# Summing most of block A's output projection in four strips, in a decode attention kernel

## The chip, the cores and the metric

The kernel runs on one core of one Trainium2 chip. The metric is the device time of one execution in microseconds (us); a value quoted for a kernel is the median of its executions. Before the change it was 1328.24 us (three executions, 1328.06 to 1329.07).

## The reference, cut to what matters

Two attention blocks with one query each. Block A reads the whole key and value caches of 32 heads; block B reads only the last 4096 keys of 8 heads, each shared by 4 query heads. Each block ends with a projection by a 4096 x 512 matrix `wo`; the results are concatenated.

```python
# A: H = 32, Sk = 32768, Dh = 128, D = 512      B: the same with 8 kv heads and a window of 4096 keys
q = (x @ wq).reshape(B, Sq, H, Dh).transpose(0, 2, 1, 3)
scores = einsum("bhqd,bhkd->bhqk", q, k_cache) * Dh ** -0.5
p = softmax(scores)
o = einsum("bhqk,bhkd->bhqd", p, v_cache)
a = o.transpose(0, 2, 1, 3).reshape(B, Sq, H * Dh) @ wo
# result: concatenate([a, b], axis=-1), 1024 values
```

Block A's caches are 32 heads x 2 x 8.39 MB in bf16. That is nearly all of the 570 MB that the kernel reads.

## The kernel before

PE is the matmul engine, DVE the vector engine, ACT the scalar engine; SP issues the loads. In this kernel the loads go to SBUF, the matmuls write to the banks of PSUM. The program gives each engine its own list of operations. An operation names the ones it depends on, and a helper turns that into semaphores. In a loop over A's 32 heads, PE transposes keys, DVE copies them out of PSUM, PE makes the scores, ACT the exponential, and PE the sum over the values. The loads are issued from SP, as soon as the buffer they go to is free. After the loop come the two projections. `wo` is loaded in parts: two for B, five for A, the last ones small so that little work is left behind the last byte.

```python
WO_CUTS = {"A": (0, 11, 19, 25, 29, 32), "B": (0, 16, 32)}     # in chunks of 128 rows of wo

def proj_part(self, name, part, out):
    a0, a1 = self.WO_CUTS[name][part:part + 2]
    oz, wo = self.c[name]["oz"], self.kbuf[:, HALF * DH * self.wo_third(name):]
    def mm(e):
        inst = None
        for a in range(a0, a1):
            inst = out(e, oz[:, a:a + 1], wo[:, 512 * a:512 * a + 512], a)
        return inst
    return self.op("pe", mm, (self.wosem[name][part], 16), self.c[name]["ozop"])   # waits for its load

def halves(self, e, bank, lhsT, rhs, begin, end):               # one chunk as two matmuls of 256 columns
    for i in range(2):
        inst = e.matmul(bank[64 * i:64 * i + 1, 0:256], lhsT=lhsT, rhs=rhs[:, 256 * i:256 * i + 256],
                        start=begin, stop=end, tile_position=(0, 64 * i), skip_group_check=True)
    return inst
```

The projection of B puts chunk `a` as one matmul of 512 columns into strip `a % 4` of a bank. It then has to add the four strips: a DVE copy of the bank to SBUF, and two f32 matmuls (four records in the trace) that sum its rows. The projection of A used the halves for every chunk, and needs no such step. (`...` marks cuts in the code of this document.)

## Time and profile before

| | before |
|---|---|
| median of 3 | 1328.24 us |
| span of the profiled execution | 1326.0 us |
| read from memory, rate over the span | 570.43 MB, 430 GB/s |
| PE, DVE, ACT busy | 73%, 57%, 4% |
| last weights landed, span ended | 1323.02, 1326.0 us |

The lines behind this table are in the prediction below. In the page, "busy" is a share of the span, and the DMA row gives tenths of each of 40 slices. In the timeline, a row is the start, the length, the engine, the source line and the operation with its count; a bracket says how long the engine stood idle before it and what ended that. Lengths of matmuls overlap: a row of 32 strips took 1.90 us, where one alone takes 0.379.

### The profile page before, as it was taken

To read this page: it belongs to the slowest core of one execution; us is meant where nothing else is said; L and a number is where in the kernel's file an instruction comes from. 1 tells how busy PE (TensorE), PEld (TensorE's weight loads), DVE (VectorE), ACT (ScalarE), POOL (GpSimd) and SP (SyncE) were. 2 spreads that over 40 slices of the span, in tenths; PEclk is the share of its full clock that TensorE was granted. 3 is DMA by queue.
4 is the path that set the end of the run, shared out by engine and by line. 5 is a ranking of instruction groups with operands and counts; after the bars stand their busy time and mean duration, and the time that the engine had idled before them with its cause. 6 is when DMAs were issued, how large, how long until landed. Compare 5 with 4: busy or idle time off the path is not lost. (4 is left out here: it accounts for less than half of the span.)

```text
span 1326.0 us, 28874 instructions
## 1 busy us (share of the span) xinstructions
PE 967.7 (73%) x13260; PEld 676.0 (51%) x13260; DVE 753.0 (57%) x1350; ACT 54.8 (4%) x167; POOL 2.2 (0%) x17
## 2 busy tenths in 40 slices
PE   4657678786777877676787767678776767877686
PEld 3445446554444655444465544455554445555453
DVE  4645456665545666554666655466655546665563
ACT  0000000000000000000000000000000000000000
POOL 0000000000000000000000000000000000000000
PEclk8878898878779887877988787898888789888888
DMA  9999999999999999999999999999999999999998
GB/s 403 445 420 427 427 431 439 437 427 435 441 427 433 435 433 433 433 437 429 435 437 429 435 435 433 431 435 437 429 433 435 435 433 433 433 431 435 435 433 351
DMA packets 13350, 570.63 MB, mean 430 GB/s; under 512 B 1812, under 2 KB 1816, under 8 KB 2200
## 3 DMA queue, kind: packets, MB, share of 16 engines
q1 hardware_dynamic: 13048, 570.44, 99.7%
q8 instruction: 9, 0.15, 0.0%
q10 hardware_dynamic: 288, 0.00, 0.0%
q14 instruction: 5, 0.04, 0.0%
HBM read 570.43 MB, written 0.00 MB: 430 GB/s over the span
## 5 line engine op out<-in xcount | busy, mean ns | idle before, releaser
L564 DVE COPY kt<-psT 128x1024 bf16<-128x1024 bf16 x1056 | 655.4, 684 | 238.9 <-PE psT L560 237.4
L560 PE MATMUL psT<-ident,kbuf 128*128 128x128 bf16 x8448 | 579.9, 234 | 170.2 <-DMA kbuf<-in_A_k_cache_dram 157.4
L560 PEld LDWEIGHTS psT<-ident,kbuf 128*128 128x128 bf16 x8448 | 540.3, 106 | 262.3 <-DMA kbuf<-in_A_k_cache_dram 165.5
L663 PE MATMUL psACC<-vbuf,ptsb 128*4 128x512 bf16 (+1 forms) x2112 | 187.5, 532 | 22.8 <-ACT ptsb L638 22.0
L583 PE MATMUL psS<-kt,qw 128*32 128x512 bf16 x2048 | 158.3, 386 | 14.8 <-DVE kt L564 14.8
L677 DVE TENSOR_SCALAR oc_A<-psACC,hot_A 128x128 f32<-128x128 f32 x32 | 11.2, 351 | 252.0 <-PE psG L690 252.0
L663 PEld LDWEIGHTS psACC<-vbuf,ptsb 128*4 128x4 bf16 (+1 forms) x2112 | 60.2, 111 | 140.3 <-issue 93.9
L611 ACT ACTIVATE psb<-psS,nb_A 128x512 bf16<-128x512 f32 x32 | 22.0, 687 | 1171.3 <-DVE nb_A L610 1171.3
L583 PEld LDWEIGHTS psS<-kt,qw 128*32 128x32 bf16 x2048 | 34.1, 95 | 57.4 <-DVE kt L564 30.4
L690 PE MATMUL psG<-oc_A,hw 128*32 128x128 f32 (+1 forms) x128 | 19.3, 227 | 52.3 <-DVE oc_A L679 52.3
L690 PEld LDWEIGHTS psG<-oc_A,hw 128*32 128x32 f32 x128 | 11.4, 109 | 62.5 <-DVE oc_A L679 55.1
L635 PE MATMUL psPT<-ident,psb 128*128 128x128 bf16 x136 | 17.9, 274 | 34.0 <-ACT psb L611 34.0
L679 DVE SCALAR_TENSOR_TENSOR oc_A<-psACC,hot_A,oc_A 128x128 f32<-128x128 f32 x96 | 33.7, 351 | 3.4
L600 DVE TENSOR_REDUCE tr_in<-psS 128x1 f32<-128x512 f32 x34 | 23.5, 692 | 17.8 <-PE psS L583 17.8
L635 PEld LDWEIGHTS psPT<-ident,psb 128*128 128x128 bf16 x136 | 10.2, 118 | 37.1 <-ACT psb L611 36.7
L604 PE MATMUL psACC<-rows,tr_in 128*1 128x64 f32 x64 | 8.7, 217 | 25.6 <-DVE tr_in L600 25.6
L638 ACT ACTIVATE ptsb<-psPT 128x512 bf16<-128x512 bf16 x34 | 20.3, 597 | 30.4 <-PE psPT L635 30.4
L604 PEld LDWEIGHTS psACC<-rows,tr_in 128*1 128x1 f32 x64 | 2.7, 81 | 35.7 <-DVE tr_in L600 35.7
L608 PE MATMUL psACC<-mr_A,nscale 1*128 1x1 f32 x64 | 12.1, 256 | 9.8 <-DVE mr_A L607 9.8
L608 PEld LDWEIGHTS psACC<-mr_A,nscale 1*128 1x128 f32 x64 | 9.4, 182 | 15.7 <-DVE mr_A L607 15.7
L610 DVE COPY nb_A<-psACC 128x1 f32<-128x1 f32 x32 | 5.0, 157 | 15.0 <-PE psACC L608 15.0
L607 DVE TENSOR_REDUCE mr_A<-psACC 1x1 f32<-1x64 f32 x32 | 6.8, 212 | 11.7 <-PE psACC L604 11.7
(80 smaller groups left out, 73.7 us busy)
## 6 DMA issues: line engine op xcount, KB each, us to landing
kbuf<-in_B_k_cache_dram SPq DMA_DIRECT2D x2, 4096.0 KB, 32.0
vbuf<-in_B_v_cache_dram SPq DMA_DIRECT2D x2, 4096.0 KB, 25.3
kbuf<-in_A_k_cache_dram SPq DMA_DIRECT2D x2, 4096.0 KB, 22.8
vbuf<-in_B_wq_dram SPq DMA_DIRECT2D x1, 4096.0 KB, 12.5
vbuf<-in_A_wq_dram SPq DMA_DIRECT2D x1, 4096.0 KB, 32.0
kbuf<-in_B_wo_dram SPq DMA_DIRECT2D x2, 2048.0 KB, 32.6
kbuf<-in_A_wo_dram SPq DMA_DIRECT2D x1, 1408.0 KB, 25.7
kbuf<-in_A_wo_dram SPq DMA_DIRECT2D x1, 1024.0 KB, 27.9
```

The costliest lines, as they stand in the source:

```text
L560: inst = e.transpose(T[:, 128 * k:128 * k + 128], src[:, DH * k:DH * k + DH], self.ident[:, :])
L564: self.copies.append(self.op("dve", lambda v: v.tensor_copy(KT[:, :], T[:, :]), o, to="pe"))
L583: inst = e.matmul(self.S[32 * c:32 * c + 32, :], lhsT=win, rhs=self.kt[(bb + c // 2) % NKT][:, 512 * (c % 2):512 * (c % 2) + 512], start=b ...
L600: o = dve(lambda v: v.reduce_max(tr["in"][:, 0:1], self.S[:, :], axis=AXX), self.sdone, self.k_pool, to="pe" if name == "A" else None)
L604: o = self.op("pe", lambda e: e.matmul(self.ACC[0:1, 0:64], lhsT=tr["in"][:, 0:1], rhs=self.rows64[:, :], start=True, stop=True, skip_grou ...
L608: o = self.op("pe", lambda e: e.matmul(self.ACC[:, 64:65], lhsT=self.nscale[:, :], rhs=t["mr"][0:1, :], start=True, stop=True, skip_group_ ...
L611: self.sread = self.op("act", lambda s: s.activation(out=self.psb[:, :], in_=self.S[:, :], func=ACTF.Exp, bias=t["nb"][:, k:k + 1], scale= ...
L635: inst = e.transpose(PT[:, 128 * jj:128 * jj + 128], self.psb[:, 128 * jj:128 * jj + 128], self.ident[:, :])
L638: self.ptread = self.op("act", lambda s: s.activation(out=self.ptsb[:, :], in_=PT[:, 0:512], func=ACTF.Copy), self.psread, to="pe")
L663: inst = e.matmul(acc[32 * c:32 * c + rows, 0:512], lhsT=lhsT, rhs=rhs, start=begin, stop=end, tile_position=(0, 32 * c), skip_group_check ...
L679: o = self.op("dve", lambda v, src=src, hot=hot: v.scalar_tensor_tensor(out=oc, in0=src, scalar=hot, in1=oc, op0=ALU.mult, op1=ALU.add), p ...
L690: return self.op("pe", lambda e: e.matmul(self.G[0:32, c0 + c:c0 + c2], lhsT=win, rhs=t["oc"][g % len(t["oc"])][:, c:c2], start=False, sto ...
```

## The change

The intent is to take matmuls out of the end of the kernel. Three quarters of A's chunks are summed in four whole-width strips as B's are, which takes one matmul per chunk instead of two. The strips are added up ahead of the last two loads, and the last seven chunks are summed in halves on top of that. One dependency in the loop is dropped as well: the exponential of a head no longer names the gather, a small operation on PE, of the head before.

```diff
@@ emit_stats: the exponential of one head
-                accum_out=t["oc"][k][:, DH:DH + 1]), o, self.psread, self.gath if g else None, to="pe")
+                accum_out=t["oc"][k][:, DH:DH + 1]), o, self.psread, to="pe")
@@ emit_proj
-        for part in range(len(self.WO_CUTS["B"]) - 1):
-            o = self.proj_part("B", part, lambda e, lhsT, rhs, a: e.matmul(
-                self.S[32 * (a % 4):32 * (a % 4) + 1, :], lhsT=lhsT, rhs=rhs, start=(a < 4), stop=(a >= 28),
-                tile_position=(0, 32 * (a % 4)), skip_group_check=True))
-        strips = self.op("dve", lambda v: v.tensor_copy(self.pb[:, :], self.S[:, :]), o)
-        o = self.op("pe", lambda e: self.halves(e, self.ACC, self.e32[:, 0:1], self.pb, True, True), strips, self.accread)
-        self.store("B", self.ACC, 512, o)
-        for part in range(len(self.WO_CUTS["A"]) - 1):
-            o = self.proj_part("A", part, lambda e, lhsT, rhs, a: self.halves(e, self.PT, lhsT, rhs, a == 0, a == 31))
+        free = None
+        for name, cut, bank, to in (("B", 2, self.S, self.ACC), ("A", 3, self.T[1], self.PT)):
+            whole = name == "B"
+            top = self.WO_CUTS[name][cut]
+            for part in range(cut):
+                o = self.proj_part(name, part, lambda e, lhsT, rhs, a, bank=bank, top=top: e.matmul(
+                    bank[32 * (a % 4):32 * (a % 4) + 1, :], lhsT=lhsT, rhs=rhs, start=(a < 4), stop=(a >= top - 4),
+                    tile_position=(0, 32 * (a % 4)), skip_group_check=True))
+            strips = self.op("dve", lambda v, bank=bank: v.tensor_copy(self.pb[:, :], bank[:, :]), o, free)
+            o = free = self.op("pe", lambda e, to=to, whole=whole: self.halves(e, to, self.e32[:, 0:1], self.pb, True, whole),
+                               strips, self.accread)
+            if whole:
+                self.store("B", self.ACC, 512, o)
+        for part in range(3, len(self.WO_CUTS["A"]) - 1):
+            o = self.proj_part("A", part, lambda e, lhsT, rhs, a: self.halves(e, self.PT, lhsT, rhs, False, a == 31))
         self.store("A", self.PT, 0, o)
```

## The prediction

> **What bounds the kernel now.** I read the page from the top: the busy shares, the 40 slices, the queues, then the chain that ended last. After that I took the stages in a table of windows, the loads with their time to landing, and the last 12 us as a timeline.
>
> ```profile
> PE 967.7 (73%) x13260; PEld 676.0 (51%) x13260; DVE 753.0 (57%) x1350; ACT 54.8 (4%) x167; POOL 2.2 (0%) x17
> ...
> DMA  9999999999999999999999999999999999999998
> ...
> HBM read 570.43 MB, written 0.00 MB: 430 GB/s over the span
> ...
> DMA 2%; PE 1%; SPq 0%; issue 0%; DVE 0%
> ```
>
> No compute engine is over 73% busy, but the DMA row is 9 in every slice except the last. The kernel reads 570 MB once, and 570.43 MB at 430 GB/s is the whole span of 1326 us. From the table of windows, the steady part:
>
> ```profile
> 45.00:1255.00 1210.00, 894.14 (x12252) 628.30 (x12251) 694.42 (x1224) 49.65 (x155) 0.00 (x0) 0.83 1.00 433
> ```
>
> Of 1210 us, PE is busy 894, DVE 694, and the DMA share is 1.00 at 433 GB/s. The loads of a head are not late either: an 8 MB key load (8.39 MB) at 433 GB/s needs 19.4 us by itself, and the view of loads gives it 27.7 us from issue to landing, a value load 26.4 us. So a load is issued 7 to 8 us before its predecessor has finished (27.7 - 19.4 and 26.4 - 19.4). Anything in the loop that is shorter than some 7 us leaves the queue full.
>
> Only the end is left, after the last byte. The chain of waits there (start, length, what):
>
> ```profile
> 1292.35 0.04 issue
> 1292.39 30.63 DMA kbuf<-in_A_wo_dram
> 1323.02 0.04 issue
> 1323.06 0.51 PE psPT L725 x6
> 1323.57 0.02 issue
> 1323.60 0.42 DVE out_sb L731
> ```
>
> The last weight load of block A is issued at 1292.39, queues behind everything else and lands at 1323.02. Six matmuls (its three chunks, two halves each), one DVE cast and the store follow; the span ends at 1326.0. The timeline shows what PE did before that:
>
> ```profile
> 1314.71 1.90 PE L738 MATMUL psS<-kbuf,oz_B 128*1 128x512 bf16 x32
> 1316.66 0.69 DVE L741 COPY pb<-psS 128x512 f32<-128x512 f32 x1 [1.65 <-PE psS L738]
> 1317.41 0.60 PE L725 MATMUL psACC<-pb,e 128*1 128x256 f32 x4 [0.80 <-DVE pb L741]
> 1317.84 2.24 PE L725 MATMUL psPT<-kbuf,oz_A 128*1 128x256 bf16 x38
> 1320.75 0.82 PE L725 MATMUL psPT<-kbuf,oz_A 128*1 128x256 bf16 x12 [0.67 <-DMA kbuf<-in_A_wo_dram]
> 1321.98 0.60 PE L725 MATMUL psPT<-kbuf,oz_A 128*1 128x256 bf16 x8 [0.41 <-DMA kbuf<-in_A_wo_dram]
> 1323.06 0.49 PE L725 MATMUL psPT<-kbuf,oz_A 128*1 128x256 bf16 x6 [0.48 <-DMA kbuf<-in_A_wo_dram]
> ```
>
> The brackets decide the case: PE stands idle 0.67, 0.41 and 0.48 us ahead of the third, fourth and fifth loads, each time for a DMA. It has already caught up with the loads, so there is no backlog for the change to shorten.
>
> [...] 32 strip matmuls took 1.90 us, one of them 0.379 us, hence (1.90 - 0.379)/31 = 49 ns each, although each has 512 columns. [...]
>
> **The change part by part.**
>
> (1) The exponential on ACT no longer names the previous head's gather among its dependencies. [...] Per head, ACT loses one wait that was long satisfied, and PE perhaps one semaphore increment. In the trace ACT starts 0.03 us after the DVE copy that releases it (copy 1303.41 + 0.16, activation 1303.60). At most 0.03 us of a head's 39 us, against 7 us of lead: zero.
>
> (2) Block B's projection: the same 32 strips, copy and halves, with unchanged flags. Zero.
>
> (3) Block A, removed: 25 chunks x 2 halves = 50 matmuls of 256 columns. They cost (2.24 - 0.272)/37 = 53 ns each, or 106 ns a chunk, 2.7 us in all. Added: 25 strips of 512 columns at 49 ns, 1.2 us; one DVE copy of 128x512 f32, 0.69 us; and four f32 half records. These took 0.60 us in B, and there the next bf16 matmul started 0.43 us after the first of them (1317.41 to 1317.84). PE records: 13260 - 50 + 25 + 4 = 13239; DVE one more, 1351.
>
> The schedule that follows, with loads landing as now. Parts 0 and 1 (19 chunks) are done by about 1319.7: the second load is in by 1318.9 (issued 1290.96, 27.9 us), and eight strips take 7 x 0.049 + 0.379 = 0.72. PE then waits about 1 us for part 2. That starts at 1320.75, and six strips end 5 x 0.049 + 0.379 = 0.62 later, at 1321.37. The DVE copy starts 0.05 later, as after B's strips, at 1321.42, and ends at 1322.11. The f32 halves start 0.06 later at 1322.17 (B: 1317.35 to 1317.41). Part 3's eight matmuls, whose weights landed at 1321.9, now stand behind them: they start at 1322.17 + 0.43 = 1322.60 instead of 1321.98. At about 50 ns each, PE is ready for part 4 at 1323.00. Part 4 lands at 1323.02 and starts at 1323.06, as now.
>
> So part 3 is **0.6 us later, and the end does not move**: the margin I work out is 0.06 us. If one of my terms is short by 0.1 us, the last six matmuls slip by some 0.05 us. Cast and store are the same instructions. Sum: 1.5 us less matmul time, none on the path; 0.7 us of copy and the halves added, just off the path or touching it by 0 to 0.2 us. Expected: +0.05 us in 1328.24, or 0.004%.
>
> **Rivals.**
>
> The copy and the f32 halves become the new wait. They put a serial step from PE to DVE to PE between part 2 and part 3, and my margin of 0.06 us is smaller than my error. If the f32 records hold PE for their whole 0.60 us rather than 0.43, part 4 starts at about 1323.2 and the time is 0.15 us more. Should the copy also start late, 0.3 us more: 1328.5.
>
> PE's clock falls. The changed kernel leaves PE idle for about 1 us before part 2 and 0.7 us during the copy. In 1300 to 1310 the granted clock was 0.68, in the last 8 us it was 1.00. Were it to fall again, matmuls on the path would take some half longer: the f32 halves, part 3 and part 4 would together slip by about 0.5 us. Against it: the tail of now has idle stretches of 0.4 to 0.8 us at 1.00. Time then: 1328.8.
>
> PE had been the bound at the end and the strips gain. That would need a backlog. The whole possible gain from PE is the stretch from landing to the last matmul's end, 0.51 us, and the change leaves those six matmuls as they are. Gain 0.
>
> The loop speeds up because ACT is released earlier. A head would have to be limited by that chain, but PE sits idle 5.06 us at the start of a head waiting for keys (the timeline around 626 us), and the DMA row has no hole. Gain 0.
>
> **Range and chances.** Every path but a broken one lies within -0.1 and +0.6 us. What is left is the spread between executions: three of the kernel before went from 1328.06 to 1329.07. I predict 1328.3 us. The range, 1327.0 to 1329.7, allows about 1 us of spread either way plus the rivals. 2% would be 26.6 us, and nothing here has that size: the whole tail behind the last load is 3 us. Faster 0.01, within 2% 0.98, slower 0.01.
>
> **What would show it right or wrong.** Right: the DMA share and the 433 GB/s of the steady part are unchanged. The chain still ends with the load of block A's last weights, six matmuls, cast and store, with the same 3.0 us from landing to end. The copy of the second strip bank starts near 1321.4 from the span's start (give or take a shift of the whole trace). Part 3's matmuls name the DVE copy or the f32 halves as what held them, no longer a DMA, and PE's idle ahead of part 4 shrinks from 0.48 us to almost nothing. Wrong in a step: the last six matmuls start more than 0.1 us after their landing (then the copy is on the path), or the granted clock in the last 6 us is below 1.00. Wrong altogether: a hole in the DMA row in the loop, which would mean that the removed wait moved the release of a buffer, or a last load that lands at another time because the queue is filled differently.

49 ns a strip comes from the 1.90 us above and 0.69 us for the copy from the trace, so 1.5 us less matmul time, none of it on the path, and 0.7 us of copy and the halves just off it come to +0.05 us. The result stays right, the runs show: wait_only, with the dropped wait alone, is correct, and so is after_again, which sums chunks 25 to 31 on top of the strips' halves. In the changed kernel's trace the gather of the head before ended 23.3 us or more before each exponential. "Some half longer" at a lower clock is the estimate, beside a clock of 0.68; in after_again, at 0.50, the last 14 matmuls took 1.70 us for 0.93.

## The result, and the profile after

The changed kernel took **1328.32 us** (six executions, 1327.73 to 1328.88), the kernel before in the same rounds 1328.66 (1328.06 to 1329.3). The ratio is **0.9997**, with a 95% interval of 0.9984 to 1.001. Ratios here divide the mean time of one kernel's fast executions by that of the other's of the same rounds, so they are not quite the ratio of the medians.

From the page of the changed kernel, the busy shares and the DMA row; then the steady part from its table of windows (busy time of PE, weight loads, DVE, ACT, POOL, then PE's granted clock as the profile gives it, 1.00 being the full one, the DMA share and GB/s):

```profile
PE 965.5 (73%) x13239; PEld 676.2 (51%) x13239; DVE 754.4 (57%) x1351; ACT 54.8 (4%) x167; POOL 2.2 (0%) x17
...
DMA  9999999999999999999999999999999999999998
```

```profile
45.00:1255.00 1210.00, 893.53 (x12263) 630.57 (x12260) 695.73 (x1225) 49.69 (x155) 0.00 (x0) 0.83 1.00 433
```

The counts are the predicted ones: PE 21 records fewer, DVE one more. In all the trace has 28802 instructions for 28874. The difference of 72 is 21 matmuls and 21 weight loads less, one copy more, and 31 waits less on ACT, one for each head but the first. The stream is as before, 433 GB/s at a share of 1.00.

The end is where the chain of waits changed (start, length, what):

```profile
1290.47 29.99 DMA kbuf<-in_A_wo_dram
1320.46 0.04 issue
1320.50 0.61 PE psT L742 x6
1321.12 0.02 issue
1321.14 0.70 DVE pb L745
1321.84 0.04 issue
1321.89 1.38 PE psPT L725 x18
1323.27 0.02 issue
1323.29 0.42 DVE out_sb L731
```

The chain no longer starts from the fifth load of A but from the **third**. Its six strips, the copy, and then 18 records in one piece: the four f32 halves, eight matmuls of the fourth load and six of the fifth. The fifth load was issued at 1291.42 and took 31.3 us, so it landed at 1322.72. PE reached its matmuls at about the same moment, since the last six take 0.5 us and end at 1323.27. From that landing to the last cast it is 0.57 us, before it was 0.58 (1323.02 to 1323.60). So the copy and the sums of the strips are on the chain now, and in this execution they cost nothing.

### The profile page after: what moved, and what is told of

The parts are those of the page before. It is cut to its first block, busy times and chain, and to the rows that moved or that the text cites. A ratio compares the mean times of both kernels' runs of the same rounds, so it can differ in the third digit from the quotient of the medians.

```text
span 1326.1 us, 28802 instructions
## 1 busy us (share of the span) xinstructions
PE 965.5 (73%) x13239; PEld 676.2 (51%) x13239; DVE 754.4 (57%) x1351; ACT 54.8 (4%) x167; POOL 2.2 (0%) x17
## 5 line engine op out<-in xcount | busy, mean ns | idle before, releaser
L663 PE MATMUL psACC<-vbuf,ptsb 128*4 128x512 bf16 (+1 forms) x2112 | 184.0, 524 | 23.0 <-ACT ptsb L638 22.0
L583 PE MATMUL psS<-kt,qw 128*32 128x512 bf16 x2048 | 157.6, 385 | 15.0 <-DVE kt L564 15.0
## 6 DMA issues: line engine op xcount, KB each, us to landing
kbuf<-in_B_wo_dram SPq DMA_DIRECT2D x2, 2048.0 KB, 33.1
kbuf<-in_A_wo_dram SPq DMA_DIRECT2D x1, 1408.0 KB, 26.3
```

Of the source, the lines that this page charges most:

```text
L583: inst = e.matmul(self.S[32 * c:32 * c + 32, :], lhsT=win, rhs=self.kt[(bb + c // 2) % NKT][:, 512 * (c % 2):512 * (c % 2) + 512], start=b ...
L663: inst = e.matmul(acc[32 * c:32 * c + rows, 0:512], lhsT=lhsT, rhs=rhs, start=begin, stop=end, tile_position=(0, 32 * c), skip_group_check ...
```

## The experiments

They came on three chips, each compared with runs of the kernel before on the same chip. The table gives all of them; "distance" is from the landing of the last weights (issue of the fifth load plus its time to landing) to the start of the last cast, in the profiled execution, and "clock" is the granted TensorE clock over that distance.

| run | median us | ratio to before (95%) | distance us | clock |
|---|---|---|---|---|
| before (first profile) | 1328.24 | | 0.58 | 1.00 |
| changed kernel (first profile) | 1328.32 | 0.9997 (0.9984 to 1.001) | 0.57 | 1.00 |
| after_again | 1329.06 | 0.9999 (0.9982 to 1.0015) | 2.12 | 0.50 |
| before_again | 1328.92 | 1.001 (0.9994 to 1.0025) | 0.58 | 1.00 |
| wait_only | 1328.19 | 0.9993 (0.9977 to 1.001) | 0.57 | 1.00 |
| few_chunks | 1328.76 | 0.9998 (0.9981 to 1.0014) | 1.78 | 0.50 |
| cut19 | 1328.55 | 0.9996 (0.9979 to 1.0012) | 1.51 | 0.50 |
| strips32 | 1329.71 | 1.0006 (0.9989 to 1.0022) | 2.50 | 0.50 |
| copies6 | 1332.97 | 1.0027 (1.001 to 1.0044) | 5.37 | 0.50 from 1324.6 |
| no_marks | 1328.28 | 0.9994 (0.9977 to 1.0011) | 2.20 | 0.50 |
| half_v | 1325.18 | 0.9969 (0.9952 to 0.9985) | 2.19 | 0.50 |
| pv_half_more | 1332.99 | 1.0026 (1.0009 to 1.0043) | 3.99 | 0.50, then 1.00 |
| pv_thrice | 1408.39, one run, state unknown | | | |
| warm | 1328.68 | 1.0002 (0.9989 to 1.0016) | 0.70 | 1.00 |

The row before_again is the yardstick: the very same kernel came out at 1.001 against itself. A microsecond is not to be seen in these times, only in traces.

### Is the copy now on the path? after_again

No edit; the changed kernel once more.

> The changed kernel once more, for a second trace of it. All theories: 1328.4 us within 1.3 us, the same as before. My theory (the last load sets the end, PE is just caught up when it lands): from the landing of the last weight load of block A to the start of the last cast 0.5 to 0.7 us, as in the kernel before (0.58). Rival (the copy and the f32 halves are now the wait): that distance is over 0.8 us in this second trace.

The time was the same, 0.9999. The trace was not; it gave the rival its number. The end of its timeline:

```profile
1319.56 1.02 PE L742 MATMUL psT<-kbuf,oz_A 128*1 128x512 bf16 x8 [2.10 <-DMA kbuf<-in_A_wo_dram]
1321.44 1.02 PE L742 MATMUL psT<-kbuf,oz_A 128*1 128x512 bf16 x6 [0.86 <-DMA kbuf<-in_A_wo_dram]
1322.50 0.69 DVE L745 COPY pb<-psT 128x512 f32<-128x512 f32 x1 [5.24 <-PE psT L742]
1323.25 1.02 PE L725 MATMUL psPT<-pb,e 128*1 128x256 f32 x4 [0.79 <-DVE pb L745]
1324.05 1.70 PE L725 MATMUL psPT<-kbuf,oz_A 128*1 128x256 bf16 x14
1325.80 0.42 DVE L731 CAST out_sb<-psPT 65x256 bf16<-65x256 f32 x1 [2.60 <-PE psPT L725]
```

The DVE copy is as long as ever, but every group of matmuls is slower: the 14 last ones took 1.70 us where the first trace of the same kernel has 0.93, the f32 records 1.02 where B's took 0.60. The table of windows says why (the columns as above; the third from the end is the granted clock):

```profile
1318.20:1319.20 1.00, 0.00 (x0) 0.00 (x0) 0.00 (x0) 0.00 (x0) 0.00 (x0) 1.00 0.97 399
1319.20:1320.20 1.00, 0.64 (x8) 0.10 (x8) 0.00 (x0) 0.00 (x0) 0.00 (x0) 0.62 1.03 420
1320.20:1322.20 2.00, 1.14 (x10) 0.10 (x6) 0.00 (x0) 0.00 (x0) 0.00 (x0) 0.50 0.95 357
```

PE had stood idle for 2.10 us waiting for A's second load, and its clock fell to 0.50. The last load landed at 1290.98 + 32.7 = 1323.68, the last cast started at 1325.80. What goes with such a fall can be read from the clock records. In the traces of the kernel before and of the changed kernel, all 268 stretches at one clock that lie within the span last a whole number of 3.413 us, to within 0.001 us. So I cut the traces into windows of that length. In the first trace of the changed kernel the clock came up at 1309.36 and fell at 1326.43, five windows later; in after_again it fell at 1319.45. Here is the last window before that, and below it the corresponding one of the first trace:

```profile
1316.04:1319.45 3.41, 1.27 (x15) 0.28 (x15) 0.52 (x2) 0.00 (x0) 0.00 (x0) 1.00 1.01 414
1316.19:1319.60 3.41, 1.85 (x23) 0.50 (x23) 0.54 (x2) 0.00 (x0) 0.00 (x0) 1.00 1.01 410
```

In after_again PE was busy for 1.27 us of the window, because A's second load landed 0.1 us after its end. In the first trace that load came in time: 1.85 us, and 1.73 in the next window. The kernel before has 2.67 and 1.91. From 60 us on, in the traces of these two kernels, all 126 windows at full clock with less than 1.63 us of work lost it, all 348 with more than 2.07 kept it, and of 15 in between 12 kept it. At half clock, none of 118 windows with less than 2.71 us brought it back, and all 124 with more than 2.73 did. Other traces agree: worked out from their timelines and tables of windows, the last 3.41 us before the fall held about 0.6 us (copies6), 0.8 (few_chunks), 1.2 (no_marks), 1.4 (cut19 and strips32) and 1.5 (pv_half_more). So the full clock of the first trace was a near thing.

What grew is not a wait for a semaphore: between the third load's landing (1321.40) and the last cast there are 4.40 us for the 2.83 of the first trace. The strips are 0.43 us longer (1.04 for 0.61) and the 18 records 1.15 (2.53 for 1.38), together the difference.

### The dropped wait alone: wait_only

```diff
-   ... o, self.psread, self.gath if g else None, to="pe")       # in the kernel before
+   ... o, self.psread, to="pe")
```

> The kernel before with the one dependency of the exponential dropped and nothing else. My theory: 1328.5 us within 1.3 us, idle of PE for key loads as before (157 us in all), and only ACT's instruction count falls, by 31. Rival (the removed wait releases ACT and with it the buffers earlier): 1 us faster or more (31 heads x 0.03 us), and loads with a longer time to landing than 27.7 and 26.4 us.

The trace has 28843 instructions, 31 fewer. The idle time of PE for key loads is 157.6 us (before 157.4), the times to landing are 27.6 and 26.3 us (27.7 and 26.4). The time is 0.9993 with an interval from 0.9977 to 1.001: the same. The rival's 1 us is smaller than this interval, so it is the unchanged waits that speak against it, not the time.

### What can a faster sum win at all? few_chunks and cut19

few_chunks sums only four chunks of each of A's first three loads (a wrong result, wrong by 32%).

```diff
-            for a in range(a0, a1):
+            for a in range(a0, a0 + 4 if name == "A" and part < 3 else a1):
```

> The changed kernel with only 4 chunks of each of block A's first three loads summed (12 instead of 25; a wrong result on purpose, all loads and waits kept). My theory: the same time, 1328.4 us within 1.3 us, because PE's sums are done while the next load is under way: what any faster sum of these chunks could win is bounded by this. Rival (PE's sums ahead of the last loads cost time): faster by the 0.6 us of 13 strips, and by more if PE had a backlog.

The time was the same (0.9998). PE spared 13 strips, waited longer instead, 2.50 us for the second load and 1.30 for the third, and fell to half clock as well:

```profile
1319.04 0.59 PE L742 MATMUL psT<-kbuf,oz_A 128*1 128x512 bf16 x4 [2.50 <-DMA kbuf<-in_A_wo_dram]
1320.93 0.59 PE L742 MATMUL psT<-kbuf,oz_A 128*1 128x512 bf16 x4 [1.30 <-DMA kbuf<-in_A_wo_dram]
```

The time alone could not show the 0.6 us at stake (its interval is 2.5 us down to 1.9 us up), and the low clock costs this run over 1 us behind the last load. It is the waits that show it: less work ahead of these loads only turns into waiting for them, so the gain of the change had nowhere to come from.

cut19 moves the sum of the strips one load forward.

```diff
-        ... ("A", 3, self.T[1], self.PT)):
+        ... ("A", 2, self.T[1], self.PT)):
-        for part in range(3, len(self.WO_CUTS["A"]) - 1):
+        for part in range(2, len(self.WO_CUTS["A"]) - 1):
```

> The changed kernel with 19 instead of 25 chunks in strips: copy and halves then stand behind the second load of block A and not the third. My theory: the same time (1328.4 us within 1.3 us), but PE waits again ahead of the last three loads (0.3 us or more ahead of the last), and the chain that ended last goes straight from the last load into its six matmuls. Rival (strips in themselves cost or save): the time moves with the number of chunks in strips.

The time was the same (0.9996), but my picture of the trace was wrong. PE did not wait ahead of the last three loads. It had waited 0.72 us for the first and 1.61 for the second load, which landed only at 1321.62; the clock fell to 0.50, the strips' sum took 1.8 us, and then all 13 chunks of the last three loads ran in one stretch of 26 matmuls in 2.98 us. The distance was 1.51 us.

### The size of the margin: copies6 and strips32

copies6 makes the copy of A's strips six times in a row.

```diff
+            for _ in range(0 if whole else 5):
+                o = self.op("dve", lambda v, bank=bank: v.tensor_copy(self.pb[:, :], bank[:, :]), o, free)
             strips = self.op("dve", ...
```

> The changed kernel with the copy of block A's strip bank made six times in a row, each waiting for the one before. My theory (the chain strips, copy, halves, part 3 already fills all the time up to the last landing): nearly all of 5 x 0.7 us shows, +3.3 to +3.8 us, so 1331.7 to 1332.2 us, and the last load waits in the buffer for as long. Rival (a wide hidden margin in front of the last load): under +1 us. Rival (the store or the drain of the queue after the last load sets the end, not PE): 0.

It took 1332.97 us where the kernel before took 1329.03 in the same rounds, +3.9 us by the medians and 1.0027 by the ratio (interval 1.001 to 1.0044, so +1.3 to +5.8 us). The first five copies took 3.59 us in the trace. In this execution the six strips still ran at full clock (0.59 us), and the clock fell to 0.50 during the copies, when PE stood idle for 4.42 us. The distance grew by 4.8 us against the first trace of the changed kernel, 3.6 for the copies and 1.2 for matmuls at half clock. So the serial step has no wide margin in front of it: what is added to it shows at the end.

strips32 puts all 32 chunks into strips.

```diff
-        ... ("A", 3, self.T[1], self.PT)):
+        ... ("A", 5, self.T[1], self.PT)):
-        ... self.halves(e, to, self.e32[:, 0:1], self.pb, True, whole)
+        ... self.halves(e, to, self.e32[:, 0:1], self.pb, True, True)
-        for part in range(3, len(self.WO_CUTS["A"]) - 1):
-            o = self.proj_part("A", part, ... halves ...)
```

> The changed kernel with all 32 chunks of block A in strips, so that copy and f32 halves stand behind the last load. My theory: landing to last cast grows from 0.58 to about 0.04 + 0.48 + 0.05 + 0.69 + 0.06 + 0.60 + 0.02 = 1.94 us, so the time by 1.4 us to 1329.8 (inside the noise of three rounds; the distance in the trace decides). Rival (the strips' lower matmul count pays): no more than 0.58 us from landing to cast.

The distance was 2.50 us where I had 1.94. The copy took its 0.69, but the clock was at 0.50: three strips took 0.61 for 0.48, and the f32 records 1.04 for 0.60. The time, 1.0006, is not clear of the noise. Behind the last load the strips cost more than the halves, as the distance shows.

### Is the load stream the bound? half_v, no_marks, pv_half_more, pv_thrice

half_v loads only half of the 17th head's values (the result is wrong, by 3.4%).

```diff
-        self.load(self.vbuf[:, :], ...[:, 0, :], ...)
+        n = HALF * DH if g == 16 else 2 * HALF * DH
+        self.load(self.vbuf[:, 0:n], ...[:, 0, 0:n], ...)
```

> The changed kernel with only half of the values of one head (the 17th) loaded, 4.19 MB less, the rest of the buffer keeping the values of the head before (a wrong result on purpose, the same instructions on the compute engines). My theory (the load stream sets the time from start to end): 4.19 MB / 433 GB/s = 9.7 us less, 1318.7 us within 1.3 us. Rival (PE and DVE set the pace, loads are just ahead): no change, 1328.4 us.

It was 3.8 us faster (1325.18 for 1328.96), not 9.7. The DMA queue's timeline around that load shows where the rest stayed:

```profile
696.08 0.33 SPq L326 DMA_DIRECT2D vbuf<-in_A_v_cache_dram  x1
714.38 0.33 SPq L326 DMA_DIRECT2D kbuf<-in_A_k_cache_dram  x1
735.64 0.33 SPq L326 DMA_DIRECT2D vbuf<-in_A_v_cache_dram  x1
```

The half load was issued at 696.08 and took 17.3 us, so it had landed at 713.4, and the next key load was issued a microsecond later: the queue had run empty. The rate was 351 GB/s from 694 to 714 and 381 from 714 to 736. Against 433 that is 20 x 82/433 + 22 x 52/433 = 6.4 us of missing stream, half a microsecond of which came back in the next window (449 GB/s over 14 us). 9.7 - 5.9 = 3.8, the difference of the medians; the agreement is loose, since the four executions lie between 1323.45 and 1326.66 and the traced one took 1326.36. The experiment was too coarse: a load that saves 9.7 us at once outruns a lead of 7. It does show how long that lead is, and that an empty queue is paid for at once.

no_marks drops sixteen tiny loads behind the last weights, and their waits.

```diff
-        for i in range(16):
-            self.load(self.marks[0:i + 1, 16 * i:16 * i + 16], self.X["A"]["wo"][0:i + 1, 0:16], self.marksem[i])
...
-        for i in range(16):
-            self.op("sp", lambda e, i=i: e.wait_ge(self.marksem[i], 16))
```

> The changed kernel without the sixteen tiny loads queued behind the last weights. The stretch from 1290 to 1314 us runs at 403 to 410 GB/s where the steady part has 433, so up to 24 x (433 - 410) / 433 = 1.3 us are missing there. My theory (the stream alone sets the end): if the tiny loads cause the gap, the last weights land 1.3 us sooner and the time is about 1327.1 us; if they do not, 1328.4. Rival (they help the last weights to land): slower than 1328.4 us.

The time was the same (0.9994), the rate from 1290 to 1314 still 402 GB/s, and the last weights landed at 1322.99. The tiny loads are not what that stretch loses; what it is stays open.

pv_half_more and pv_thrice give PE more to do in every head: half of the value matmuls twice, or all of them three times.

```diff
-            for c, lhsT, rhs, begin, end in todo:
+            for c, lhsT, rhs, begin, end in (todo[:32] if name == "A" else []) + todo:      # pv_half_more
+            for c, lhsT, rhs, begin, end in (todo * 2 if name == "A" else []) + todo:       # pv_thrice
```

> The changed kernel with the first 32 of the 64 value matmuls of every head of block A made twice (the result stays right): 32 x 92 ns = 2.9 us more on PE per head, 94 us over 32 heads. My theory (a value load is issued 7 us before its predecessor has landed, and PE idles 5 us per head): hidden, 1328.4 to 1331 us. Rival (the release of the buffers in the loop is on the path, so the dropped wait could have mattered too): +94 us or a good part of it.

> The same with all 64 matmuls made three times: 128 x 92 ns = 11.8 us more per head. My theory: more than the 5.06 us that PE idles per head and the 7 us of lead, so the loop is bound by PE: (11.8 - 5.06) x 32 = 216 us more, about 1544 us (1480 to 1600, as the granted clock may change), with holes in the DMA row. Rival (loads keep their lead whatever PE does): under 1350 us.

The total wait of PE for key loads (us in total, times, longest) in the kernel before, in pv_half_more and in pv_thrice:

```profile
PE psT L560 <- DMA kbuf<-in_A_k_cache_dram: 157.4, 31, 12.5
```

```profile
PE psT L560 <- DMA kbuf<-in_A_k_cache_dram: 104.6, 30, 12.7
```

```profile
PE psT L560 <- DMA kbuf<-in_A_k_cache_dram: 12.3, 1, 12.3
```

In pv_half_more the value matmuls were busy 243.8 us for 187.5, 56 us more, and the wait for keys shrank by 53: the added work went into idle time. The time rose by 4.0 us (1332.99 for 1328.98), above what I had expected and far below a rival's +94. Of that I can place a part: in its trace the last weights landed at 1325.03, some 1.5 us later than usual, and PE, late with the last head's doubled matmuls and partly at half clock, needed 3.99 us from there to the last cast.

In pv_thrice the wait for keys is gone, the DMA row has a hole (8 in its fourth slice; the mean is 406 GB/s), and the loop is PE's: 1408 us. My 1544 was too much, because I had counted 92 ns for a value matmul. That was a matmul partly at half clock (0.72 from 652.26 to 657.25, where the kernel before has 64 of them). With PE busy the clock rose (mean 0.891 for 0.833), and 192 of them took about 13 us in the heads I looked at, where 64 had taken 4.9 to 6.3.

### Keeping the clock up: before_again and warm

By now the question was whether the strips bring the low clock, or an execution brings it whatever the kernel. before_again is the kernel before, unchanged. warm is the changed kernel with idle matmuls, the result of which nobody reads:

```diff
+                if not whole:
+                    self.op("pe", lambda e, n=(20, 20, 10)[part]: self.filler(e, n))
...
+    def filler(self, e, n):                       # into a bank that nobody reads any more
+        for a in range(n):
+            inst = e.matmul(self.T[2][32 * (a % 4):32 * (a % 4) + 1, :], lhsT=self.c["B"]["oz"][:, a:a + 1],
+                            rhs=self.kbuf[:, 512 * a:512 * a + 512], start=True, stop=True, ...)
+        return inst
```

> The kernel before once more, for a second trace of its end. In six traces with the strips (the second of the changed kernel among them) PE's granted clock fell to 0.50 some 4 us before the last weights landed, and the way from landing to last cast grew from 0.57 to about 2.1 us; in the two traces without strips it stayed at 1.00. Theory (the fewer and faster matmuls leave PE idle for too long): here the clock stays at 1.00 up to the last cast, landing to cast 0.6 us. Rival (the clock falls by chance in either kernel): 0.50 and about 0.9 us here too.

> The changed kernel with idle matmuls into a spare bank: 20 after block A's first load, 20 after its second and 10 during the strip copy (1.0, 1.0 and 0.5 us at 49 ns; the result stays right). Theory: PE's clock stays at 1.00 to the end, landing to last cast is 0.5 to 0.7 us again, the time 1328.0 us within 1.3 us, so at most 1 us or so better than the changed kernel and not clear of the noise; the distance in the trace decides. Rival (the idle matmuls only delay the sums, or the clock falls anyway): landing to cast over 1 us.

From before_again's table of windows and then from warm's timeline:

```profile
1320.30:1322.30 2.00, 1.25 (x20) 0.56 (x16) 0.00 (x0) 0.00 (x0) 0.00 (x0) 1.00 0.54 189
1322.30:1324.30 2.00, 1.09 (x14) 0.44 (x14) 0.42 (x1) 0.00 (x0) 0.00 (x0) 1.00 0.07 15
```

```profile
1323.01 0.60 PE L725 MATMUL psPT<-pb,e 128*1 128x256 f32 x4
...
1323.44 0.93 PE L725 MATMUL psPT<-kbuf,oz_A 128*1 128x256 bf16 x14
1324.41 0.42 DVE L731 CAST out_sb<-psPT 65x256 bf16<-65x256 f32 x1 [1.46 <-PE psPT L725]
```

before_again kept its clock; the distance is 0.58 us again. warm had its clock at 1.00 from 1317 to the end, and its 14 last matmuls took 0.93 us: 0.70 us of distance for 2.12. PE was busy for 2.62 and 3.27 us of its last two windows. Added work alone, useless work even, gave 1.4 us back; with the windows of after_again this points to too little work in a window as the cause of the low clock. It is one trace, and its past differs: its clock had been at 0.50 from 1313.35 to 1316.76, where B's 32 strips took 3.32 us for 1.90. In the time nothing is to be seen of it (1.0002, interval 0.9989 to 1.0016), and no version with a right result beats both kernels clear of the noise.

**What stays open.** The executions differ in more than the clock. From the issue of A's first weights to the landing of the last it is 32.0 to 32.4 us in the three traces without strips and 32.8 in copies6, but 33.1 in the changed kernel's first trace and 34.4 to 35.2 in after_again, few_chunks, no_marks, half_v, warm, cut19 and strips32 (31.6 in pv_half_more, where PE was late). In these seven PE is up to 2 us further ahead of the loads, so it waits longer. The GB/s row differs too: even (mostly 427 to 441) in the first four, swinging between about 410 and 443 in the others. half_v was even up to its hole and swung after it, so this can change within an execution. Whether the halves would keep the clock up in such an execution no trace shows. An estimate says yes, narrowly: 22 halves take 21 x 0.053 + 0.272 = 1.39 us where the 11 strips of A's first load took 0.81, which would lift the 1.27 us of after_again's window to some 1.85. Why the loads fall into one rhythm or the other was not tried.

## Why the prediction was right

- **The bound is the load stream.** It holds. 56 us of added matmuls cost 4 us, and the DMA share is 1.00 before and after. The test by a smaller load was blunted, because the queue ran empty.
- **A lead of 7 us in the loop, so the dropped wait is worth nothing.** It holds: 31 waits fewer, the same waits for loads. A saving of 9.7 us in one load emptied the queue, which agrees with a lead of 7.
- **No backlog ahead of the last loads, so fewer matmuls win nothing.** It holds: in few_chunks the work taken out came back as waiting for the loads. Its time, within 2.5 us, is too coarse to show it.
- **The schedule behind the third load.** I had 0.62 us for the strips, a copy from 1321.42 to 1322.11, and PE ready for the last load with 0.06 us to spare. The first trace has 0.61, a copy from 1321.14, and no gap and no delay. The prediction's sign that the chain would still end with the last load failed: the chain goes back to the third one, because the two ways end together. Its sign of a wrong step, a clock below 1.00 in the last 6 us, came in after_again.
- **The clock as a rival.** Named, but set aside on the wrong evidence and mis-sized. I held the kernel before's idle stretches against it (0.4 to 0.8 us at 1.00), and counted 1 us of idling before the third load. What told the traces apart was not the length of one stretch but the work in a whole window of 3.41 us: 2.67 and 1.91 us in the last two of the kernel before, 1.27 in after_again's. The strips also left PE idle ahead of the second load, 0.99 us in the first trace and 2.10 in the second, which I had not worked out. And I put 0.5 us on it; with the strips, the f32 records and the last 14 matmuls all on the chain it is 1.5 us in the distance.
- **The range.** 1328.3 us against 1328.32 measured. That closeness is luck: a second set of executions gave 1329.06, and single executions of one kernel are spread over more than 2 us. Luck, too, is the full clock of the first trace, which had 1.85 and 1.73 us of work in its last two windows, where 1.63 is the least that kept the clock and 2.07 the most that lost it. That the verdict is "same" follows from the sizes: 3 us in all lie behind the last load.

## What to carry to other kernels

Before speeding up work at a kernel's end, read what ended the idle time in front of it. Where each bracket names a load, as here with 0.41 to 0.67 us, the work is already hidden, and making it shorter only made the engine wait longer (2.50 us for the second load in few_chunks, 0.99 and 2.10 in the two traces of the changed kernel). On PE that had a price of its own here: each of 126 windows of 3.41 us with less than 1.63 us of work lost half its clock, so in after_again the serial steps still ahead ran at half clock (1.70 us for 0.93) just when nothing hid them. Compare two traces of the same kernel before explaining a microsecond.
